# Which queue issues the two transfers that regroup the keys: SyncE or GpSimd

## The chip, the cores and the metric

The kernel runs on one core of a Trainium2 chip. The core's engines work side by side, each through its own list of instructions in order: TensorE (PE, with its weight loads PEld), VectorE (DVE), ScalarE (ACT), GpSimd (POOL) and SyncE (SP), which here only issues transfers. Any of SyncE, ScalarE and GpSimd can issue a transfer (DMA); an issue that has to wait holds up all that stands behind it on its engine. The metric is the device time in microseconds of one execution, of which the span from the first to the last instruction is nearly all.

## What is computed

A decaying linear attention, whose output goes through two gated feed-forward layers (the second behind an RMS norm). The core of the reference:

```python
# attention: q, k, v, a_re, a_im are (4, 8, 768, 48)
mag = np.sqrt(a_re * a_re + a_im * a_im)
scale = np.minimum(mag, 0.999) / (mag + 1e-06)
a_re_n, a_im_n = (a_re * scale, a_im * scale)
for t in range(S):
    ar, ai = (a_re_n[:, :, t, :, None], a_im_n[:, :, t, :, None])
    new_re = ar * S_re - ai * S_im
    new_im = ar * S_im + ai * S_re
    kv = np.einsum('bhd,bhe->bhde', k[:, :, t], v[:, :, t])
    S_re, S_im = (new_re + kv, new_im)
    y[:, :, t] = np.einsum('bhd,bhde->bhe', q[:, :, t], S_re)
# a layer: x (3072, 384), w_gate and w_val (384, 1536), w_out (1536, 384), float64 in memory
g = x @ w_gate
silu = g * (1.0 / (1.0 + np.exp(-g)))
return (silu * (x @ w_val) @ w_out).astype(np.float32)
# the second layer's x is first x / sqrt(mean(x * x) + 1e-06) * rms_g
```

## The kernel before, in words

The 768 steps are cut into 6 blocks of 128, the 8 heads into pairs: 24 groups of one block and two heads, numbered block by block. Two groups that follow one another are a pair and share their decays. For a pair, `e1` and `scan` turn a_re and a_im (tile `aar`) into running products of the decays; for a group, `e2a` and `e2b` multiply the queries (`qt`) and the keys divided by the products (`kt`, L664, on VectorE). ScalarE makes the logarithms and exponentials for this (L488, L489, L631, L632), and the copies of transposes.

On TensorE a group is `pe_att`: transposes of kt and qt (`tp`, L689), scores (`sp`, L704), the output (`yp`, L721 and L726) and, as late work behind the next group's scores, the new state (`zp`, L745 and L747). For zp the keys are wanted with time on the partitions. `regroup` makes that: it stores kt to a scratch tensor `kd` in HBM (L672, two buffers) and loads it in the other order into `ktok` (L673, one buffer). kd waits for kt; ktok waits for kd to land and for the zp that read ktok before. The values `vt` (two buffers) are loaded at L453, the output goes by L736 from `yt` into `xf`.

When the four groups of a block are done, `layer1` runs the first feed-forward layer for its 512 columns: projections (`gv`, L361, 9 matmuls each), Silu on ScalarE (`h`, L370), product on VectorE (L384), rounding and remainder (`hh` L385, `hl` L393), and the output (`acc`, L797). Each weight tile comes by L328 into `wraw`, is narrowed from float64 by VectorE (L59 to L61) and split into two parts by ScalarE, in the first layer with TensorE's help (`wl`, L336 and L337). The second layer (`o`, L921) follows for all 3072 rows, its weights being loaded and narrowed while the last block's first layer runs.

The order is set in two steps. The tables T_E1 to T_WF at the top give each task a due time, and `in_order` lists the pieces by it. A scheduler then places each instruction on its engine's list by an estimate of when its operands are there; so a change of one transfer's engine can move instructions on all engines. ScalarE needs another table for Silu than for logarithm and exponential; a table load is set in wherever the list goes from one to the other. Before the change every transfer is issued by SyncE, but for the stores of x1d (L805) and two of the last outputs, which ScalarE issues. GpSimd fills masks at the start (up to L313) and one tile of ones between the layers (L955).

Of the kernel before, what the change touches and what calls it, by code (L numbers as in the profile page):

```python
# [261 lines left out]
def decay_attention_two_ffn(ctx: ExitStack, tc: tile.TileContext, q, k, v, a_re, a_im,  # L262
                            wg, wv, wo, w2g, w2v, w2o, rms_g, out):
    nc = tc.nc
    V, A, T, G, SY = nc.vector, nc.scalar, nc.tensor, nc.gpsimd, nc.sync
# [23 lines left out]
    with ExitStack() as fast:  # L289
# [346 lines left out]
        def e2b(i, s):  # L636
            gr = groups[i]
            b = gr.blk
            U, C, el = b.U, b.C, b.el
            half = i % 2  # L640
            o = {}

            def qq(c):
                def go():
                    if c == 0:
                        o["q"] = ap1.tile([128, 4 * G2 * 2 * D], F32, tag="qt", name="qt", bufs=BUFS["qt"])[:, :2 * el].rearrange(
                            "p (u g c d) -> p u g c d", u=U, g=G2, c=2)
                        o["k"] = ap1.tile([128, 4 * G2 * 2 * D], F32, tag="kt", name="kt", bufs=BUFS["kt"])[:, :2 * el].rearrange(
                            "p (u g c d) -> p u g c d", u=U, g=G2, c=2)
                        qkn[i] = (o["q"], o["k"])  # L650
                    V.tensor_tensor(o["q"][:, :, :, c, :], qk[i][:, 0, :el].rearrange("p (g u d) -> p u g d", g=G2, u=U),
                                    s["a"][:, c].rearrange("p u (g d) -> p u g d", g=G2), op=ALU.mult)
                return go

            def nw():
                m2, w0, t = s["q2"][:, 0], s["q2"][:, 1], s["tt"][:, 768:768 + el]
                V.tensor_tensor(t, m2, w0, op=ALU.mult)
                V.scalar_tensor_tensor(w0, t, 2.0, w0, op0=ALU.subtract, op1=ALU.mult)
                wv_ = w0.rearrange("p (u g d) -> p u g d", g=G2, u=U)
                V.tensor_tensor(wv_, wv_, qk[i][:, 1, :el].rearrange("p (g u d) -> p u g d", g=G2, u=U), op=ALU.mult)  # L660

            def kk(c):
                def go():
                    V.tensor_tensor(o["k"][:, :, :, c, :], s["q2"][:, 1].rearrange("p (u g d) -> p u g d", g=G2, u=U),  # L664
                                    s["a"][:, c].rearrange("p u (g d) -> p u g d", g=G2), op=ALU.mult)
                return go

            def regroup():
                kt = ap2.tile([128, B, G2, 2, D], F32, tag="ktok", name="ktok", bufs=BUFS["ktok"])
                ktok[i] = kt  # L670
                kd = dram.tile([128, U, G2 * 2 * D], F32, tag=f"kd{U}", name="kd", bufs=2)
                SY.dma_start(out=kd, in_=o["k"].rearrange("p u g c d -> p u (g c d)"))  # L672
                SY.dma_start(out=kt[:C].rearrange("p b g c d -> p b (g c d)"),  # L673
                             in_=kd.rearrange("(b r) u x -> (r u) b x", b=B))

            return [(1, qq(0)), (1, qq(1)), (3, nw), (1, kk(0)), (1, kk(1)), (0.1, regroup)]

        def pe_att(i):
# [351 lines left out]
```

## Time and profile before

| | us |
|---|---|
| median of 3 runs (1218.2 to 1222.41) | 1219.62 |
| the profiled execution | 1217.24 |
| its span | 1215.5 |
| TensorE busy in the span | 1133.2 |
| VectorE, ScalarE, GpSimd busy | 777.0, 672.3, 1.5 |
| mean granted TensorE clock | 0.986 of full |

Durations in rows come from the profiled execution. In a row of waits stand the engine and line that waited, whom for, the total in us, how often and the longest; the one waited for is the one that came last. In a row of a timeline stand the start in us, the time in us, engine, line, operation, operands, and the idle time ahead in square brackets with what ended it. A row of the windows gives one stretch.

### The profile page before, as it was taken

Reading aid. Unit: us, or ns where it says so; the run is one execution under the profiler, and the core shown is the slowest. Engines: PE = TensorE matmul, PEld = TensorE weight load, DVE = VectorE, ACT = ScalarE, POOL = GpSimd, SP = SyncE. Lnnn points to the kernel's source line nnn. Section 1 sums busy time; section 2 is a strip of 40 time slices with the busy share of each in tenths; the row PEclk is TensorE's granted clock in tenths of the full one; section 3 lists DMA queues with packets and bytes.
Section 4 is the critical chain, followed back from the end, with each engine's and each line's share of the span. In section 5 each row is a group of like instructions: output and inputs, shape, how many; then the busy total and the mean of one; then the engine's idle time right before and its main releaser. Section 6 shows DMA issues by size and latency. Waiting matters only on the chain.

```text
span 1215.5 us, 16686 instructions
## 1 busy us (share of the span) xinstructions
PE 1133.2 (93%) x6098; PEld 944.7 (78%) x6098; DVE 777.0 (64%) x1711; ACT 672.3 (55%) x1167; POOL 1.5 (0%) x12
## 2 busy tenths in 40 slices
PE   2468979999999999999999999999999999999997
PEld 1246767788888888888878877888888888888886
DVE  5988999989888697888754488842432424224222
ACT  5666979876677656675364688742421424214211
POOL 0000000000000000000000000000000000000000
PEclk9988989999999999999999999999999999999998
DMA  6255454442423224222313244400010000000000
GB/s 168 85 145 143 116 154 141 123 118 66 119 76 90 75 60 123 57 82 70 95 59 98 79 130 145 129 26 28 1 52 1 26 27 1 26 1 1 27 1 29
DMA packets 105514, 90.84 MB, mean 75 GB/s; under 512 B 34000, under 2 KB 92368, under 8 KB 105424
## 3 DMA queue, kind: packets, MB, share of 16 engines
q1 hardware_dynamic: 102544, 84.58, 24.4%
q10 hardware_dynamic: 2880, 5.11, 1.1%
q8 instruction: 50, 0.82, 0.3%
q14 instruction: 40, 0.33, 0.1%
HBM read 66.06 MB, written 18.87 MB: 70 GB/s over the span
## 4 chain that ended last, share of the span: by engine, by line
PE 72%; ACT 11%; DVE 8%; DMA 4%; issue 2%; SPq 1%; ACTq 0%; DVEq 0%
PE gv L361 39%; PE o L921 12%; PE acc L797 8%; PE sp L704 4%; PE tp L689 3%; DMA wraw<-in_moe_w_gate_dram 2%; ACT T L695 2%; PE zp L745 2%; PE yp L721 2%; PE yp L726 1%; ACT L425 1%; ACT T L692 1%; DMA wraw<-in_moe_w_val_dram 1%; SPq L430 1%; ACT w L332 1%
## 5 line engine op out<-in xcount | busy, mean ns | idle before, releaser
L361 PE MATMUL gv<-xh,w 128*128 128x512 f32 x1728 | 569.2, 394 | 0.3 <-ACT h L370 0.3
L361 PEld LDWEIGHTS gv<-xh,w 128*128 128x128 f32 x1728 | 324.2, 188 | 67.8 <-ACT h L370 1.3
L361 PE MATMUL gv<-xl,w 128*128 128x512 f32 x864 | 339.1, 393 | 0.0
L384 DVE TENSOR_TENSOR gv<-h,gv 128x512 f32<-128x512 f32 (+1 forms) x145 | 100.1, 691 | 217.0 <-PE gv L361 211.3
L370 ACT ACTIVATE h<-gv 128x512 f32<-128x512 f32 x144 | 85.9, 597 | 185.2 <-PE gv L361 184.6
L361 PEld LDWEIGHTS gv<-xl,w 128*128 128x128 f32 x864 | 162.5, 188 | 31.4 <-issue 0.5
L385 ACT ACTIVATE hh<-gv 128x512 fp32r<-128x512 f32 (+1 forms) x145 | 85.7, 591 | 158.5 <-DVE gv L384 157.8
L393 DVE TENSOR_TENSOR hl<-gv,hh 128x512 fp32r<-128x512 f32 (+1 forms) x145 | 99.3, 685 | 103.1 <-PE o L921 70.8
L797 PE MATMUL acc<-hh,w 128*128 128x512 f32 x432 | 148.5, 398 | 2.6 <-ACT hh L385 2.6
L921 PE MATMUL o<-w,hh 128*128 128x384 f32 x576 | 146.5, 337 | 0.4 <-ACT x1s L803 0.4
L921 PEld LDWEIGHTS o<-w,hh 128*128 128x128 f32 x576 | 105.6, 188 | 5.9 <-ACT x1s L803 0.7
L921 PE MATMUL o<-w,hl 128*128 128x384 f32 x288 | 96.8, 340 | 0.9 <-DVE hl L393 0.9
L797 PEld LDWEIGHTS acc<-hh,w 128*128 128x128 f32 x432 | 80.3, 188 | 21.0 <-ACT hh L385 4.1
L797 PE MATMUL acc<-hl,w 128*128 128x512 f32 x216 | 86.3, 399 | 0.7 <-DVE hl L393 0.4
L336 PE MATMUL wl<-wy,ident 128*128 128x384 f32 x72 | 39.6, 639 | 42.3 <-DVE wy L61 30.7
L695 ACT ACTIVATE T<-tp 96x512 f32<-96x512 f32 x48 | 52.7, 1097 | 42.6 <-PE tp L689 42.1
L704 PEld LDWEIGHTS sp<-T,T 96*128 96x128 f32 x384 | 51.4, 204 | 22.8 <-ACT T L692 21.4
L704 PE MATMUL sp<-T,T 96*128 96x128 f32 x384 | 57.4, 296 | 9.6 <-ACT T L692 9.3
L921 PEld LDWEIGHTS o<-w,hl 128*128 128x128 f32 x288 | 53.5, 188 | 2.9 <-DVE hl L393 2.9
L336 PEld LDWEIGHTS wl<-wy,ident 128*128 128x128 f32 x72 | 14.2, 231 | 50.8 <-DVE wy L61 36.1
L370 ACT ACT_TABLE_LOAD x38 | 48.8, 1283 | 3.4 <-PE gv L361 2.7
L797 PEld LDWEIGHTS acc<-hl,w 128*128 128x128 f32 x216 | 40.6, 188 | 11.0 <-DVE hl L393 2.9
(134 smaller groups left out, 1502.3 us busy)
## 6 DMA issues: line engine op xcount, KB each, us to landing
wraw<-in_moe_w_gate_dram SPq DMA_DIRECT2D x24, 384.0 KB, 3.6
wraw<-in_moe_w_val_dram SPq DMA_DIRECT2D x24, 384.0 KB, 3.4
wraw<-in_moe_w_out_dram SPq DMA_DIRECT2D x24, 384.0 KB, 3.2
kd<-kt SPq DMA_DIRECT2D x24, 384.0 KB, 2.5
ktok<-kd SPq DMA_DIRECT2D x24, 384.0 KB, 3.6
aar<-in_a_re_dram SPq DMA_DIRECT2D x48, 96.0 KB, 2.4
aar<-in_a_im_dram SPq DMA_DIRECT2D x48, 96.0 KB, 2.7
qk<-in_q_dram SPq DMA_DIRECT2D x96, 48.0 KB, 2.3
```

Of the source, the lines that this page charges most:

```text
L336: T.matmul(ps[:, :384], ident, y, start=True, stop=False)
L361: T.matmul(ps[:, :N], w[:, a, i + c, :], x()[b][:, c, :N], start=(n == 0), stop=(n == 8))
L370: A.activation(h[:, :N], st[f, 0][:, :N], AF.Silu)
L384: V.tensor_tensor(t[:, z], st[f, "h"][:, z], st[f, 3][:, z], op=ALU.mult)
L385: A.activation(hh[:, z], t[:, z], AF.Copy)
L393: V.tensor_tensor(hl[:, z], st[f, "t"][:, z], st[f, "hh"][:, z].bitcast(F32), op=ALU.subtract)
L689: T.transpose(ps[0:96, u * 128:u * 128 + 128], s[:, u, h].rearrange("p c d -> p (c d)"), ident)
L695: A.activation(t[:, :N].rearrange("p (b r u) -> p u b r", u=U, b=B), ps[0:96, :N].rearrange("p (u b r) -> p u b r", u=U, b=B), AF.Copy)
L704: T.matmul(ps[:C, bb * C:bb * C + C], o[h, 1][:, bb], o[h, 0][:, :, bb, :], start=True, stop=True)
L721: T.matmul(dst, vt[i][:C, col:col + 64], o[h, "p"][:C, bb * C:bb * C + C].rearrange("p (u r) -> p u r", u=U), start=True, stop=not inter)
L797: T.matmul(acc[e][:, :N], w[:, a, 6 + e, :], hs_[c][:, :N], start=(f == 0 and n == 0), stop=(f == NF - 1 and n == 2))
L921: T.matmul(acc[m][:, :DM], hs_[c][:, m * 128:m * 128 + 128], w[:, a, 6:9, :].rearrange("p c e -> p (c e)"), start=(f == 0 and x == 0), sto ...
```

## The change

Both transfers of `regroup` are put on GpSimd's queue (G) in place of SyncE's (SY).

```diff
                 kd = dram.tile([128, U, G2 * 2 * D], F32, tag=f"kd{U}", name="kd", bufs=2)
-                SY.dma_start(out=kd, in_=o["k"].rearrange("p u g c d -> p u (g c d)"))
-                SY.dma_start(out=kt[:C].rearrange("p b g c d -> p b (g c d)"),
+                G.dma_start(out=kd, in_=o["k"].rearrange("p u g c d -> p u (g c d)"))
+                G.dma_start(out=kt[:C].rearrange("p b g c d -> p b (g c d)"),
                              in_=kd.rearrange("(b r) u x -> (r u) b x", b=B))
```

The scheduler places instructions anew. SyncE's list is the same up to the loads of the queries for group 2, where the first kd and ktok stood. Before (x2, x3, x4 are the batches of one load; aar belongs to the pair of groups 4 and 5):

```order
L328 DMA wraw<-in_moe_w_val_dram 128x3x256
L430 DMA qk<-in_q_dram 32x2x192 x2
L672 DMA kd<-kt 128x768
L430 DMA qk<-in_q_dram 32x2x192 x2
L430 DMA qk<-in_k_dram 32x2x192
L673 DMA ktok<-kd 128x4x192
L430 DMA qk<-in_k_dram 32x2x192 x3
L430 DMA aar<-in_a_re_dram 32x4x192 x4
L430 DMA aar<-in_a_im_dram 32x4x192 x2
L736 DMA xf<-yt 48x512 x2
```

The same place on SyncE with the change:

```order
L328 DMA wraw<-in_moe_w_val_dram 128x3x256
L430 DMA qk<-in_q_dram 32x2x192 x4
L430 DMA qk<-in_k_dram 32x2x192 x4
L430 DMA aar<-in_a_re_dram 32x4x192 x4
L430 DMA aar<-in_a_im_dram 32x4x192 x4
L736 DMA xf<-yt 48x512 x2
```

The two transfers of the keys are gone from it, and all eight loads of the decays stand ahead of the store of xf. On GpSimd, between the last mask and the memset of L955, the pairs of kd and ktok now stand, 24 of each (the first rows):

```order
L313 AFFINE_SELECT mask_100<-mask_100 128x128
L672 DMA kd<-kt 128x768
L673 DMA ktok<-kd 128x4x192
L672 DMA kd<-kt 128x768
L673 DMA ktok<-kd 128x4x192
```

Before, L955 came right behind that mask. On ScalarE the third place is the exponentials of group 17, near the end of a block's first layer. Before:

```order
L623 ACTIVATE e2t<-an 128x768
L425 ACT_TABLE_LOAD
L631 ACTIVATE e2t<-e2t 128x384
L803 ACTIVATE x1s<-acc_3951 128x4x128
L632 ACTIVATE e2t<-e2t 128x384
```

And with the change:

```order
L370 ACT_TABLE_LOAD
L370 ACTIVATE h<-gv 128x512
L425 ACT_TABLE_LOAD
L385 ACTIVATE hh<-gv 128x512
L370 ACT_TABLE_LOAD
L370 ACTIVATE h<-gv 128x512
L631 ACT_TABLE_LOAD
L631 ACTIVATE e2t<-e2t 128x384
L385 ACTIVATE hh<-gv 128x512
L632 ACT_TABLE_LOAD
```

Silu (L370) now falls between the steps of the group's logarithm and exponential, with a table load at each turn. In the whole program ScalarE has 88 table loads before and 100 with the change.

## Rows read from the trace of the kernel before

**Rows 1.** The page: each engine's busy time, its share of the span, its instructions.
```profile
PE 1133.2 (93%) x6098; PEld 944.7 (78%) x6098; DVE 777.0 (64%) x1711; ACT 672.3 (55%) x1167; POOL 1.5 (0%) x12
```

**Rows 2.** Windows: stretch, length, busy PE, PEld, DVE, ACT, POOL; clock, DMA share, GB/s
```profile
0.00:45.00 45.00, 9.37 (x15) 4.14 (x15) 31.87 (x89) 26.39 (x56) 1.32 (x11) 1.00 0.44 115
45.00:210.00 165.00, 135.07 (x730) 102.39 (x729) 149.57 (x372) 126.34 (x267) 0.00 (x0) 0.92 0.48 139
210.00:635.00 425.00, 420.30 (x2662) 348.01 (x2661) 351.40 (x843) 284.74 (x406) 0.00 (x0) 1.00 0.32 89
635.00:765.00 130.00, 126.45 (x576) 103.03 (x575) 86.89 (x167) 89.49 (x204) 0.20 (x1) 1.00 0.37 112
765.00:1215.50 450.50, 441.96 (x2124) 387.16 (x2122) 157.31 (x243) 145.33 (x236) 0.00 (x0) 0.99 0.07 23
```

**Rows 3.** Waits of TensorE from 45 to 210 us: total, times, longest.
```profile
PE tp L689 <- DVE kt L664: 7.0, 4, 3.1
PE wl L336 <- DVE wy L61: 6.6, 5, 2.4
PE tp L689 <- DVE X L462: 5.9, 1, 5.9
```

**Rows 4.** Waits of TensorE from 210 to 640 us.
```profile
PE sp L704 <- ACT T L692: 3.7, 12, 0.6
PE tp L689 <- ACT T L695: 0.6, 2, 0.3
```

**Rows 5.** Waits of SyncE's queue over the whole span.
```profile
SPq L328 <- DVE wy L61: 138.4, 51, 14.5
...
SPq L673 <- PE zp L747: 93.0, 19, 14.4
SPq L672 <- DVE kt L664: 49.0, 15, 11.3
```

**Rows 6.** Timeline of SyncE's queue, 47 to 71 us.
```profile
47.99 0.35 SPq L672 DMA_DIRECT2D kd<-kt  x1
...
50.64 0.38 SPq L673 DMA_DIRECT2D ktok<-kd  x1
...
69.53 0.90 SPq L430 DMA_DIRECT2D aar<-in_a_im_dram  x2
```

**Rows 7.** Groups of VectorE's instructions by form: count, busy us, mean ns of one.
```profile
L783 DVE TENSOR_TENSOR xl<-xf,xh 128x512 fp32r<-128x512 f32 x18 | 12.2, 685 | 0.5 <-ACT xh L782 0.5
...
L494 DVE TENSOR_TENSOR e1w<-e1w,an 128x768 f32<-128x768 f32 x12 | 11.4, 952 | 3.8 <-ACT e1w L493 3.8
```

**Rows 8.** Timelines of SyncE's queue and TensorE, 315 to 330 us.
```profile
315.73 0.38 SPq L673 DMA_DIRECT2D ktok<-kd  x1
316.16 1.06 SPq L453 DMA_DIRECT2D vt<-in_v_dram  x2
...
329.07 0.80 PE L745 MATMUL zp<-vt,ktok 128*96 128x48 f32 x8
```

**Rows 9.** Groups of ScalarE's instructions, 210 to 640 us: count, busy us, mean ns.
```profile
L370 ACT ACT_TABLE_LOAD x27 | 34.6, 1283 | 3.2 <-PE gv L361 2.7
L425 ACT ACT_TABLE_LOAD x24 | 30.8, 1283 | 0.4
```

**Rows 10.** DMA issues: count, KB each, median us from issue to landing.
```profile
kd<-kt SPq DMA_DIRECT2D x24, 384.0 KB, 2.5
ktok<-kd SPq DMA_DIRECT2D x24, 384.0 KB, 3.6
```

**Rows 11.** Timelines: VectorE's keys of group 11, and TensorE's transposes of them.
```profile
320.63 1.02 DVE L664 TENSOR_TENSOR kt<-e2t,an 128x384 f32<-128x384 f32 x2
322.06 0.60 PE L689 MATMUL tp<-ident,kt 128*96 128x128 f32 x4
```

**Rows 12.** Groups of VectorE's instructions: L59 and L60, mean ns of one.
```profile
L59 DVE TENSOR_SCALAR wy<-wraw 128x384 uint32<-128x384 uint32 x72 | 25.5, 356 | 16.3 <-DMA wraw<-in_moe_w_gate_dram 12.6 <-DMA wraw<-in_moe_w_out_dram 2.4 <-DMA wraw<-in_moe_w_val_dram 0.9
L60 DVE SCALAR_TENSOR_TENSOR wy<-wraw,wy 128x384 uint32<-128x384 uint32 x72 | 39.8, 555 | 0.8
```

## The prediction

> **What bounds the kernel now.** I read the profile from the outside in: the windows by stage, the waits of TensorE in the stages where it idles, then the waits of the queue that loses the two transfers. TensorE is busy 441.96 of the last 450.50 us and 420.30 of the 425 us between 210 and 635 us; it idles 35.6 us before 45 us, 29.9 us between 45 and 210 us and 3.6 us between 635 and 765 us [rows 2]. So the end is set by TensorE's own work plus what it loses in the first 210 us. In 45 to 210 us VectorE is busy 149.57 of 165 us and ScalarE 126.34 [rows 2]: TensorE there waits for what VectorE and ScalarE make, the keys (7.0 us on L664, and 5.9 us in one piece that the view names after X at L462, which ends beside L664), and the narrowed weights (6.6 us) [rows 3]. After 210 us the largest are 3.7 and 0.6 us [rows 4]. No row of TensorE's waits names a transfer. GpSimd has 1.5 us of work in the whole span [rows 1], all but 0.2 us of it in the first stage [rows 2].
>
> SyncE is another matter: it waits much. L673 waited 93.0 us for zp, in 19 pieces, and L672 49.0 us for the keys; but L328 waited 138.4 us for VectorE to free a weight buffer [rows 5]. A queue that waits is not a queue that is late: what counts is who needs the transfers behind it.
>
> **The change part by part.** *The issues.* SyncE loses 24 issues of 0.35 us and 24 of 0.38 us [rows 6], 17.5 us in all, and the waits ahead of them; the same 48 transfers go to GpSimd, where nothing else is queued between the masks and the memset of L955. That memset and the test of the flag after it now stand behind the last ktok; the memset's reader is the second layer's first norm, behind the whole last block of the first layer: nothing.
>
> *What moves up behind them.* The first kd stood at 47.99 and the first ktok at 50.64 us; the loads behind them move up by their issue and wait, some 2.3 us, and the two a_im loads that stood at 69.53 us, behind an xf store, now stand ahead of it, right behind the first two [rows 6]. That lets VectorE take the next pair's e1 steps earlier, but it takes them ahead of nearer work: in the new order L494 and L499 (0.95 us each, by L494's row) stand before the keys of group 2, and one L783 (0.69 us) behind [rows 7]: +1.2 us. Counted in the same way for group 3 it is +0.6, for group 4 +2.0, for group 5 -0.4, for groups 6 and 7 -0.2 us and for group 8 nothing different. VectorE works in order and is over 90% busy, so the sum of work ahead of the keys is when they come. The loss at group 4 is inside the 5.9 us for which TensorE later waits for group 5 anyway [rows 3], and at group 5 VectorE is level again. By this engine the first stage costs **-0.2 us**.
>
> *A wait stays where it was.* The ktok load of 315.73 us is followed at once by the vt loads and the xf stores [rows 8]. Those wait for the same group's matmuls and copies: vt's buffer is free only when yp and zp have read it, and xf needs yt. So SyncE still stops near there, now at L453 or L736; of 93.0 us of waiting most changes its name. I count no gain from it, because TensorE waits for no load.
>
> *The activation tables.* The order is built with other arrival times, and ScalarE's instructions fall differently: 100 table loads against 88 in all the program. One costs 1283 ns [rows 9]. One of the twelve stands ahead of the exponentials of group 4 (counted up to its L632), a second ahead of group 6's; ten come from group 14 on, most of them after 400 us, where Silu now falls between the logarithm and the exponential. The first two are 2.6 us on an engine that is 77% busy in that stage [rows 2]: all of it if ScalarE is the later of the two engines, nothing if VectorE is. I take the middle of -0.2 and +2.6, **+1.2 us**. The ten later ones are 12.8 us on an engine busy 284.74 of 425 us; at the upper end all of it delays TensorE, at the lower nothing. The 51 loads that stand in 210 to 640 us now [rows 9] live beside TensorE waits of 4.3 us [rows 4], 0.08 us for each, and this row is the nearest: 10 x 0.08 = **+0.8 us**.
>
> *The transfer by GpSimd.* No row shows a transfer that GpSimd issues. From SyncE kd lands in 2.5 and ktok in 3.6 us [rows 10]. Who waits for them: ktok is needed by zp alone (L745), and its single buffer is free only when the zp before it is done. The closest pair of zp: the ktok between them is issued at 315.73 us, would land at 319.3 us, and zp reads it at 329.07 us [rows 8]; 9.7 us are to spare, and at the other 18 pairs more. Faster landing gains nothing, and slower landing costs nothing up to 9.7 us more. Above that each further microsecond is paid at up to 19 places. I take **0**; the other end is a rival below. The Trainium skill (DMA: Bandwidth & Descriptors, Specifications) gives about 1 us to the first byte on the GpSimd path and 0.6 us on the SyncE path; as an estimate from that page 48 x 0.4 = 19 us if every transfer were on the path, and nothing by the slack above. No run here shows either latency.
>
> **The sum.** 1.2 + 0.8 = +2.0 us. The profiled execution took 1217.24 us, 1215.5 of it the span, so 1219.2 us by it; the median of the three runs shown is 1219.62 us, 2.4 us above the profiled one. On the scale of the median: 1219.6 + 2.0 = **1221.6 us**. A measurement of this kernel can tell about 0.3%, 3.7 us, from no change; the forecast lies within it.
>
> **The rivals.**
> *Slower, by the order.* The keys come hardly ahead of their transposes: group 11's end at 321.65 us and are read at 322.06 [rows 11]. Up to there TensorE has under half a microsecond in hand at most groups, so a chain of ScalarE that gets 2.6 us longer can reach TensorE several times, and the ten later loads stand in front of Silu, whose product TensorE needs next. With all of the twelve loads on the path it is 15.4 us; a third to a half of that, 5 to 8 us, is what I would expect if this happens: 1225 to 1230 us, say 1227. For it: the count of loads, and two engines that are 91 and 77% busy beside each other up to 210 us. Against it: from 330 us on TensorE has work of the first layer in its own queue between the groups, and hardly waits now. It decides once loads that follow one another delay Silu beyond what TensorE holds between a projection and its product.
>
> *Slower, by GpSimd.* A transfer whose issue to landing on GpSimd takes over 3.6 + 9.7 = 13.3 us stops TensorE at the closest zp, and the next ones after it. At 15 us it would be under 2 us at each of a few pairs, at most 10 us in all: about 1230 us. A second form lies on VectorE. L59 takes 356 ns for 384 elements and L60 555 ns for as many [rows 12], so L59 runs in a faster form than its neighbours; if that form and GpSimd's writing of descriptors shut each other out, VectorE stands still in the stage in which it is the bound: 14 transfers before 210 us, with 0.4 us (one L59) at each, are 5 us of VectorE and up to 1226 us. The Trainium skill (SBUF — State Buffer, section SBUF: two separate sides, the box on the "DVE blocks DMA" trap) states that GpSimd can't write descriptors while VectorE runs an operation that uses both of its ports, and in its section Who interferes with whom that whoever comes second waits for the whole instruction. The trace agrees only so far as L59's 356 ns go; no row has both engines at work.
>
> *Faster.* SyncE without 48 issues and two waits for each group brings loads forward at a place where the chain needs them. A weight load may stand behind a ktok that waits for zp, as the vt loads do [rows 8]. If the narrowed weights come earlier, the 6.6 us in L336's row shrink, and the 5.9 us before group 5 may as well: 4 to 8 us of the 29.9 us, 1212 to 1216, say 1214 us. Against it: VectorE is busy 91% of that stage, and earlier data don't make it faster.
>
> **How the numbers follow.** Forecast, within 0.3% (1216 to 1223.3 us): 0.44. Slower by the order: 0.32. Slower by GpSimd: 0.09. Faster: 0.15. So faster 0.15, same 0.44, slower 0.41. The range for 8 in 10 leaves about one in ten at either end: the lower end cuts the faster rival near its price, 1214.5; the upper takes in twice the middle price of the slower ones, 1231. The likeliest case alone has 1216 to 1223.3.
>
> **What would show it.** ScalarE's table loads in the new profile (88 to 100 in the program, fewer executed) and TensorE's waits after 210 us: below 6 us the forecast holds, over 10 us the first rival. DMA issues: kd and ktok under 10 us from issue to landing, and no wait of L745 for ktok. SyncE's waits: L673 and L672 gone, L453 and L736 larger. VectorE: a mean of L59 of 356 ns as before; 500 ns or more would be the shut-out. TensorE's idle time in 45 to 210 us: 29.9 us, give or take 3. A granted clock other than 0.92 there would add a cause that I don't count: TensorE ran for parts of that stage at the lower level.

## The result, and the profile with the change

| | before | with the change |
|---|---|---|
| median, us (runs) | 1218.91 (4) | 1228.76 (4) |
| lowest and highest, us | 1216.65, 1222.41 | 1228.2, 1230.14 |
| ratio, 95% interval | | 1.0083 (1.0067 to 1.0099) |
| span of the profiled execution, us | 1215.5 | 1227.0 |

The change costs 9.9 us. That lies inside the range of the prediction (1214.5 to 1231 us), but not where its forecast lay (1221.6 us, within 0.3%); it is nearest to the first rival, "slower, by the order", which was put at 1227 us.

First the row of the page on the engines, which answers [rows 1], and the windows that answer [rows 2] (columns as there):

```profile
PE 1138.7 (93%) x6098; PEld 944.9 (77%) x6098; DVE 777.3 (63%) x1711; ACT 691.1 (56%) x1179; POOL 33.3 (3%) x60
```

```profile
45.00:210.00 165.00, 134.43 (x717) 100.27 (x715) 147.55 (x367) 128.70 (x267) 8.57 (x13) 0.92 0.50 139
210.00:635.00 425.00, 416.27 (x2594) 341.99 (x2594) 348.90 (x840) 292.99 (x410) 21.87 (x33) 1.00 0.30 85
```

GpSimd has 48 instructions more and 31.8 us more work; ScalarE has 12 more (the table loads) and 18.8 us more. TensorE has as many matmuls as before and 5.5 us more busy time. In the first stage its idle time is 30.6 us (29.9 before) at the same granted clock of 0.92.

The waits of TensorE from 210 to 640 us, which answer [rows 4] (columns: who waits, for whom, us in total, times, longest):

```profile
PE sp L704 <- ACT T L692: 5.9, 14, 1.6
PE gv L361 <- ACT h L370: 1.6, 1, 1.6
PE tp L689 <- ACT T L695: 0.6, 2, 0.3
PE gv L361 <- ACT xh L782: 0.5, 1, 0.5
PE acc L797 <- DVE hl L393: 0.2, 1, 0.2
```

Together 8.8 us, and all but 0.2 of it for ScalarE. Before it was 4.6 us: the 4.3 us of [rows 4] and one row more of the same view of the kernel before:

```profile
PE gv L361 <- ACT h L370: 0.3, 1, 0.3
```

The waits of SyncE's queue over the whole span, which answer [rows 5], and the issues of the two transfers, which answer [rows 10]:

```profile
SPq L328 <- DVE wy L61: 154.3, 53, 14.3
...
SPq L453 <- PE zp L747: 106.8, 19, 13.3
SPq L736 <- ACT yt L728: 69.4, 13, 29.2
```

```profile
kd<-kt POOLq DMA_DIRECT2D x24, 384.0 KB, 3.0
ktok<-kd POOLq DMA_DIRECT2D x24, 384.0 KB, 4.6
```

The waits of L673 and L672, 142.0 us, are gone. The 106.8 us of L453 are new, and L736 waits 27.1 us longer for yt (42.3 before): nearly the whole wait stayed and changed its name.

**Where the time went** is not read from these sums. The kernel has a mark that says it better: when a block's first layer is done, ScalarE copies the first part of acc out (L803). The first of these rows, of the kernel before and with the change:

```profile
253.84 1.10 ACT L803 ACTIVATE x1s<-acc 128x512 f32<-128x512 f32 x1 [0.43 <-PE acc L797]
```

```profile
256.69 1.11 ACT L803 ACTIVATE x1s<-acc 128x512 f32<-128x512 f32 x1 [0.44 <-PE acc L797]
```

The distance from one such mark to the next is a block's length. In kernels whose lists are alike in a block it agrees to about 0.1 us in the second, third and fifth block (the second: 107.39, 107.45, 107.40, 107.45 and 107.49 us in five of the kernels of the table), so it tells far smaller things than a timed run. The sixth is less steady (77.5 to 78.4 us with the lists of before), and so is the fourth with the lists of the change (110.0 us, and 109.1 in e2). The first block's end is not steady either: with the lists of the kernel before it fell between 252.4 and 254.0 us in four profiles, with those of the changed kernel between 254.5 and 256.7 us in five. The table gives the marks of all kernels, worked out from the rows of L803 of their timelines; the experiments follow in the next section. The marks are those of one execution, the ratio is that of all; for e8, e9 and e10 the execution with the marks was the slowest.

| kernel | 1st ends | 2nd | 3rd | 4th | 5th | 6th | ratio, 95% interval |
|---|---|---|---|---|---|---|---|
| before | 253.8 | 107.4 | 105.1 | 106.4 | 102.2 | 77.9 | 1 |
| with the change | 256.7 | 108.4 | 106.4 | 110.0 | 103.6 | 78.8 | 1.0083 (1.0067 to 1.0099) |
| e1 lists of before, GpSimd issues | 254.0 | 107.5 | 105.1 | 106.4 | 102.1 | 77.8 | 1.0008 (0.9995 to 1.0021) |
| e2 lists of the change, SyncE issues | 255.2 | 108.5 | 106.4 | 109.1 | 103.6 | 78.0 | 1.0079 (1.0066 to 1.0092) |
| e3 ScalarE's list of before alone | 259.8 | 107.6 | 105.0 | 106.4 | 102.2 | 77.6 | 1.0046 (1.0028 to 1.0063) |
| e4 change, six places mended | 254.6 | 108.4 | 106.1 | 106.5 | 103.6 | 77.6 | 1.0049 (1.0033 to 1.0066) |
| e5 e1, twelve table loads added | 252.4 | 107.4 | 110.7 | 115.2 | 103.9 | 78.1 | 1.0127 (1.0104 to 1.0149) |
| e6 before, three places mended | 253.3 | 107.8 | 105.0 | 105.9 | 102.1 | 77.5 | 0.9996 (0.9983 to 1.0008) |
| e7 change up to the first mark | 255.1 | 107.5 | 105.1 | 106.3 | 102.2 | 78.2 | 1.0029 (1.0017 to 1.0040) |
| e8 e1, SyncE's list of the change | 269.6 | 107.5 | 105.1 | 106.5 | 102.1 | 78.4 | 1.0106 (1.0087 to 1.0126) |
| e9 only ktok on GpSimd | 266.0 | 109.9 | 104.2 | 106.4 | 102.1 | 78.2 | 1.0093 (1.0076 to 1.0109) |
| e10 only kd on GpSimd | 268.3 | 114.6 | 102.3 | 106.4 | 102.2 | 77.6 | 1.0132 (1.0106 to 1.0158) |
| e11 e4, one Silu earlier | 254.5 | 108.2 | 106.1 | 106.4 | 103.6 | 77.5 | 1.0045 (1.0030 to 1.0059) |
| e12 e7, weight loads ahead | 256.8 | 107.5 | 105.1 | 106.3 | 102.2 | 78.2 | 1.0024 (1.0015 to 1.0032) |

With the change 2.8 us are lost up to the first mark of this profile, and 1.0, 1.3, 3.6, 1.4 and 0.9 us in the blocks behind it; the second layer adds 0.4 us. In e2, with the same lists, the fourth block loses 2.7 us and the sixth 0.1. The second layer, 462.6 to 463.6 us in the other profiles, takes 464.9 us in e2 and 465.2 in e9; why is open.

### The profile page after: what moved, and what is told of

Its sections match the earlier page's. It is cut to its first block, busy times and chain, and to the rows that moved or that the text cites. A ratio compares the mean times of both kernels' runs of the same rounds, so it can differ in the third digit from the quotient of the medians.

```text
span 1227.0 us, 16726 instructions
## 1 busy us (share of the span) xinstructions
PE 1138.7 (93%) x6098; PEld 944.9 (77%) x6098; DVE 777.3 (63%) x1711; ACT 691.1 (56%) x1179; POOL 33.3 (3%) x60
## 3 DMA queue, kind: packets, MB, share of 16 engines
q0 software_dynamic: 4608, 18.88, 4.5%
## 4 chain that ended last, share of the span: by engine, by line
PE 69%; ACT 13%; DVE 9%; DMA 5%; issue 2%; SPq 1%; ACTq 0%; DVEq 0%
PE gv L361 37%; PE o L921 12%; PE acc L797 8%; PE sp L704 4%; ACT T L695 3%; DMA wraw<-in_moe_w_gate_dram 2%; PE zp L745 2%; PE tp L689 2%; PE yp L721 2%; PE yp L726 1%; ACT T L692 1%; ACT L370 1%; ACT L425 1%; DMA wraw<-in_moe_w_val_dram 1%; ACT h L370 1%
## 5 line engine op out<-in xcount | busy, mean ns | idle before, releaser
L384 DVE TENSOR_TENSOR gv<-h,gv 128x512 f32<-128x512 f32 (+1 forms) x145 | 100.0, 690 | 226.8 <-PE gv L361 206.2
L370 ACT ACTIVATE h<-gv 128x512 f32<-128x512 f32 x144 | 85.8, 596 | 175.8 <-PE gv L361 175.0
L336 PE MATMUL wl<-wy,ident 128*128 128x384 f32 x72 | 39.4, 636 | 42.8 <-DVE wy L61 30.3
L695 ACT ACTIVATE T<-tp 96x512 f32<-96x512 f32 x48 | 52.7, 1098 | 21.7 <-PE tp L689 21.0
L336 PEld LDWEIGHTS wl<-wy,ident 128*128 128x128 f32 x72 | 14.1, 229 | 51.1 <-DVE wy L61 36.8
```

The source lines that it names most:

```text
L336: T.matmul(ps[:, :384], ident, y, start=True, stop=False)
L370: A.activation(h[:, :N], st[f, 0][:, :N], AF.Silu)
L384: V.tensor_tensor(t[:, z], st[f, "h"][:, z], st[f, 3][:, z], op=ALU.mult)
L695: A.activation(t[:, :N].rearrange("p (b r u) -> p u b r", u=U, b=B), ps[0:96, :N].rearrange("p (u b r) -> p u b r", u=U, b=B), AF.Copy)
```

## The experiments

The change does two things at once: it gives two transfers to another engine, and it makes the scheduler place instructions anew on every list. The first theory (A) was that the new places cost the time and the issue by GpSimd costs nothing; the rival (B) that GpSimd's transfers cost it, by later landing or by standing in VectorE's way. To part them, the order of an engine's list was held by edges between neighbours that set the order of issue and wait for nothing. This stands at the end of the kernel's body; a table gives each list by the place of its instructions in the text:

```python
            _row = [_mine[j + o] for j, o in enumerate(_off)]
            for _x, _y in zip(_row, _row[1:]):
                tc.add_manual_dep(_y, _x.name, mybir.DependencyInfo(
                    mybir.DependencyClass.NoSync, mybir.DependencyReason.DATA), reason="order")
```

The traces have 84 table loads in the kernel before and 96 with the change; the prediction's 88 and 100 are those in the program, of which four did not run.

### One half at a time

**e1**: GpSimd issues, the lists of before.

```diff
-                SY.dma_start(out=kd, ...
-                SY.dma_start(out=kt[:C]...
+                G.dma_start(out=kd, ...
+                G.dma_start(out=kt[:C]...
...
+ORDER = {"PE": <before>, "DVE": <before>, "Activation": <before>, "SP": <before, less the 48>, ...}
```

> GpSimd issues both transfers of the keys, as in the changed kernel, but the order of TensorE's, VectorE's, ScalarE's and SyncE's other instructions is held at that of the kernel before, by edges that set order of issue alone. Theory A (the new order of the lists costs the time, the issue by GpSimd nothing): the time of the kernel before, ratio 1.000, within 0.3%, 84 to 88 table loads, and ktok's landing still near 4.6 us. Theory B (the transfers on GpSimd cost it: later landing, or VectorE hindered while GpSimd describes them): ratio about 1.008, as the changed kernel. A share of each would lie between, by its size.

Measured: 1.0008 (0.9995 to 1.0021), no difference that can be told, and each block as long as before to 0.1 us. ktok landed in 4.3 us.

**e2**: SyncE issues, the lists of the change.

```diff
                 SY.dma_start(out=kd, ...
                 SY.dma_start(out=kt[:C]...
...
+ORDER = {"PE": <change>, "DVE": <change>, "Activation": <change>, "SP": <change, with the 48 put in>}
```

> The other half: SyncE issues both transfers, as in the kernel before, but the order of TensorE, VectorE, ScalarE and of SyncE's other transfers is held at that of the changed kernel; the two transfers stand on SyncE's list where the changed program as a whole has them. Theory A (order): ratio 1.008, 1.005 to 1.011, TensorE's waits for T L692 and h L370 as in the changed kernel (12.7 and 1.6 us). Theory B (GpSimd): ratio 1.000, within 0.3%.

Measured: 1.0079 (1.0066 to 1.0092), the whole loss without one transfer on GpSimd. The waits are those of the change, too: 12.4 us for T at L692 over the span, 1.6 us for h at L370. Theory B falls; what remains is which of the new places cost the time.

**e3**: GpSimd issues, ScalarE's list alone is held.

```diff
+ORDER = {"Activation": <before>}
```

> GpSimd issues both transfers, ScalarE's list alone is held at the order of the kernel before, and with it its number of table loads; the scheduler is free in the rest. Theory A1 (within the order it is ScalarE's list, with its twelve more table loads, that costs the time): ratio 1.000 to 1.003. Theory A2 (the moved instructions of TensorE and VectorE cost it, the table loads lie hidden or cost the 2.0 us that the prediction gave them): ratio 1.005 to 1.008. Theory B (GpSimd): 1.008.

Measured: 1.0046 (1.0028 to 1.0063), between the two. The blocks tell why. From the first mark on they are as long as before: with ScalarE's list of before the scheduler makes nearly the other lists of before as well (221 of 1711 places differ on VectorE, and none of TensorE's behind 311 us). The whole loss, 5.9 us in this profile, lies ahead of the first mark, where most of those differences are. It did not come in every execution: five of the six took 1223.3 to 1223.9 us and one 1217.34, and why is open. So the later blocks follow from ScalarE's list, but the experiment doesn't say whether by its table loads or by other places. ScalarE's list of the one kernel with TensorE's and VectorE's of the other would say it; there is no such run.

### What a table load costs

In the fourth block of the changed kernel ScalarE's timeline reads (columns: start us, us, engine, line, operation):

```profile
477.36 1.28 ACT L370 ACT_TABLE_LOAD   x1
...
479.27 1.28 ACT L425 ACT_TABLE_LOAD   x1
...
481.18 1.28 ACT L370 ACT_TABLE_LOAD   x1
...
483.09 1.28 ACT L631 ACT_TABLE_LOAD   x1
...
485.42 1.28 ACT L632 ACT_TABLE_LOAD   x1
...
487.14 1.08 ACT L695 ACTIVATE T<-tp 96x512 f32<-96x512 f32 x1
488.24 1.28 ACT L370 ACT_TABLE_LOAD   x1
489.54 0.60 ACT L370 ACTIVATE h<-gv 128x512 f32<-128x512 f32 x1
490.03 0.58 ACT L692 ACTIVATE T<-tp 96x512 f32<-96x512 f32 x1
```

Six loads in 12.2 us, with no idle time between the rows, and the copies of the transposes (T, L695 and L692) at the end of the row. TensorE's timeline at the same place:

```profile
488.43 0.61 PE L797 MATMUL acc<-hh,w 128*128 128x512 f32 x2
490.67 1.16 PE L704 MATMUL sp<-T,T 96*128 96x128 f32 x8 [1.62 <-ACT T L692]
```

It ran out of work of the layer and stopped for 1.62 us until L692 was done.

**e4** puts six such places right: a Silu that stands between the logarithm and the exponential goes behind, or the load goes behind the Silu. The third of the six, on ScalarE's list:

```diff
-L370 ACT_TABLE_LOAD
-L370 ACTIVATE h<-gv 128x512
-L425 ACT_TABLE_LOAD
-L385 ACTIVATE hh<-gv 128x512
-L370 ACT_TABLE_LOAD
-L370 ACTIVATE h<-gv 128x512
-L631 ACT_TABLE_LOAD
-L631 ACTIVATE e2t<-e2t 128x384
-L385 ACTIVATE hh<-gv 128x512
-L632 ACT_TABLE_LOAD
+L370 ACTIVATE h<-gv 128x512
+L385 ACTIVATE hh<-gv 128x512
+L370 ACTIVATE h<-gv 128x512
+L425 ACT_TABLE_LOAD
+L631 ACTIVATE e2t<-e2t 128x384
+L385 ACTIVATE hh<-gv 128x512
 L632 ACTIVATE e2t<-e2t 128x384
```

> GpSimd issues, and all lists stand as in the changed kernel, but for six places on ScalarE's list in the blocks from the third on: where a Silu (L370) stands between a table load or logarithm and the exponential that belongs to it, the Silu is put behind the exponential, or the load behind the Silu. That takes 14 table loads out (96 to 82). Theory A1 (the table loads between them cost the loss after the first block, 0.4 to 0.7 us each where ScalarE's copies are what TensorE waits for): ratio 1.000 to 1.004. Theory A2 (the loads lie hidden at the 0.08 us each of the prediction, other moves in the lists cost the time): ratio 1.006 to 1.008. The loss in the first 254 us, 2.8 us, should stay in either.

Measured: 1.0049 (1.0033 to 1.0066), a gain of 0.0034 or 4.1 us on the change, between the two forecasts. The blocks show that both were right in different places. The fourth block, 110.0 us with the change, is 106.5, level with the kernel before: its loss was the table loads there, together with the places of Silu that make them needed (the edit takes both away). The change has 20 loads in this block, e4 has 11 and the kernel before 14: the six new ones cost 3.6 us (2.7 in e2), 0.45 to 0.6 us each, and going three below the number of before gains nothing more. The third block loses three loads and gains 0.3 us. The fifth has four loads more with the change than before; e4 takes two of them out and the block stays as long. The second, where no load was added, keeps its 1.0 us. The sixth is 1.2 us shorter, but that one isn't steady. The same place with the edit:

```profile
477.46 0.60 ACT L370 ACTIVATE h<-gv 128x512 f32<-128x512 f32 x1 [0.70 <-PE gv L361]
478.08 1.28 ACT L425 ACT_TABLE_LOAD   x1
479.38 0.53 ACT L631 ACTIVATE e2t<-e2t 128x384 f32<-128x384 f32 x1
480.25 0.60 ACT L385 ACTIVATE hh<-gv 128x512 fp32r<-128x512 f32 x1 [0.34 <-DVE gv L384]
```

ScalarE now waits for the others at two of the four rows, where it had a queue of work before.

**e5** adds loads and moves nothing: at the six pairs that the change tears apart, Silu's table and then the other's are loaded once more.

```diff
             pre = A.preload_act_table_set("natural_log_exp_and_others")
...
+            if len(calls) - 1 in TWICE:
+                pair = [A.preload_act_table_set(x).ins for x in ("silu_and_others", "natural_log_exp_and_others")]
```

> GpSimd issues, all lists stand as in the kernel before, and at the six pairs that the changed kernel tears apart two more table loads (Silu's and back) are set ahead of the logarithm: twelve loads more, nothing moved. Theory A1: 0.4 to 0.7 us a load, ratio 1.004 to 1.007 against the kernel before. Theory A2 (hidden, 0.08 us a load): ratio 1.001, not told from the first experiment's 1.0008.

Measured: 1.0127 (1.0104 to 1.0149), 14.5 us above e1 and far above both theories: 1.2 us for each load of 1.28 us, as if nothing hid them. The profile has a second cost in it, in the fourth block. Right ahead of the third mark ScalarE loads three tables in a row (the edit moves the lines of this kernel on by one to seven; L789 is L782 elsewhere):

```profile
466.13 1.28 ACT L427 ACT_TABLE_LOAD   x1
467.42 2.57 ACT L431 ACT_TABLE_LOAD   x2
```

A split of x (xh, here L789) comes late behind them, TensorE stops, and what it does next is slow. Its timeline, then the windows from there, of the third block and of the fourth (column before the last two: the granted clock):

```profile
473.54 2.01 PE L361 MATMUL gv<-xh,w 128*128 128x512 f32 x4 [2.29 <-ACT xh L789]
```

```profile
473.50:478.00 4.50, 4.46 (x13) 3.55 (x14) 1.71 (x4) 3.85 (x5) 0.56 (x1) 0.62 0.55 208
...
359.77:470.43 110.66, 108.26 (x681) 90.43 (x680) 86.12 (x206) 76.48 (x101) 5.30 (x8) 1.00 0.28 79
470.43:585.63 115.20, 108.11 (x650) 89.37 (x649) 87.54 (x208) 75.13 (x103) 5.28 (x8) 0.96 0.25 69
```

Four matmuls take 1.80 us up to the next row at 475.34, 0.45 us each, where at full clock one takes 0.23: the lower of the two levels, 1.2 GHz. In the fourth block the loads' price is thus mixed with the clock's. The third block has six of the twelve loads at full clock and is 5.6 us longer than in e1, the fifth has two and is 1.8 us longer: 0.9 us a load. At these places most of a load's time reaches the end, and a stop of TensorE can cost more than its length.

**e6** takes loads out of the kernel before, which has three such places of its own (six loads); SyncE issues.

```diff
 L631 ACTIVATE e2t<-e2t 128x384
-L370 ACT_TABLE_LOAD
-L370 ACTIVATE h<-gv 128x512
-L632 ACT_TABLE_LOAD
-L632 ACTIVATE e2t<-e2t 128x384
+L632 ACTIVATE e2t<-e2t 128x384
+L370 ACT_TABLE_LOAD
+L370 ACTIVATE h<-gv 128x512
```

> SyncE issues, all lists as in the kernel before, but for three places on ScalarE's list where the kernel before too has a Silu between a logarithm and its exponential: the Silu goes behind. Six table loads less (84 to 78). Theory A1: 2.4 to 4.2 us less, ratio 0.9965 to 0.998. Theory A2: 0.5 us less, ratio 1.000, within 0.1%.

Measured: 0.9996 (0.9983 to 1.0008). Six loads less, 7.7 us of ScalarE, give at most 2 us and by the middle of the interval 0.5. With two loads less in each of three blocks, the fourth gains 0.6 us, the third nothing, and the second loses 0.4. By the whole time the loads lay hidden here, as theory A2 said. The price of a load is thus one of its place: none that can be told here, about 0.5 us in the fourth block of the change, 0.9 us in e5.

The Trainium skill (ScalarE: Activation LUTs, Table sets: the hidden batching unit) says to batch activations by table set rather than by function. The fourth block of e4 agrees, 3.5 us shorter than with the change; e6 shows the rule kept better than before and no gain that can be told.

**e11** tests the second block, which has no more loads than before and is 1.0 us longer. Its profile has one large wait, for a Silu that stands behind three steps of the attention. On ScalarE's list of e4:

```diff
 L692 ACTIVATE T_2507<-tp 96x512
+L370 ACT_TABLE_LOAD
+L370 ACTIVATE h<-gv 128x512
 L623 ACTIVATE e2t<-an 128x768
 L695 ACTIVATE T_2521<-tp 96x4x128
-L370 ACT_TABLE_LOAD
-L370 ACTIVATE h<-gv 128x512
```

> The changed kernel with the six places mended, and one Silu more moved: the first Silu of the second block, which stands behind three copies and Squares of the attention in the changed kernel and made TensorE wait 1.59 us, is put ahead of two of them. If the place of that Silu makes the second block longer (108.4 us in place of 107.4): block back to 107.2 to 107.7 and ratio 1.0035 to 1.0045. If not, block at 108.4 and ratio 1.0049 as without it.

Measured: the block has 108.2 us in place of 108.4, ratio 1.0045 (1.0030 to 1.0059). The theory falls. TensorE's timeline with the change, then in e11:

```profile
267.84 0.50 PE L361 MATMUL gv<-xh,w 128*128 128x512 f32 x1 [1.59 <-ACT h L370]
```

```profile
267.69 0.50 PE L797 MATMUL acc<-hh,w 128*128 128x512 f32 x1 [1.63 <-ACT hh L385]
```

The wait for h is gone, and 1.63 us for hh stand in its place a few matmuls on. In e11 hh waited 0.22 us for VectorE's product (L384). The product's row in e11, then in the kernel before:

```profile
266.32 0.69 DVE L384 TENSOR_TENSOR gv<-h,gv 128x512 f32<-128x512 f32 x1
```

```profile
261.84 0.69 DVE L384 TENSOR_TENSOR gv<-h,gv 128x512 f32<-128x512 f32 x1
```

In e11 h is done at 263.27 us, and the product stands on VectorE's list behind L626, an L507 and the two L651 of the next queries. In the kernel before h is done at 261.61 us, the product follows at once, and L651 comes 4 us later. So VectorE's new order is a candidate for this block, with ScalarE's; no experiment moved it, and what makes the block longer stays open.

### The first block

**e7** holds the lists of the change up to the first mark and those of before from there.

```diff
+ORDER = {"PE": <change up to the first L803, then before>, "DVE": <same>, "Activation": <same>, ...}
```

> GpSimd issues, the lists stand as in the changed kernel up to the end of the first block's layer (254 us), and as in the kernel before from there. If the loss of each stretch is its own and nothing is given back later: the 2.8 us of the first stretch and no more, ratio 1.002 to 1.0035. If the profile of the changed kernel misled on the first stretch and all loss belongs to the later blocks: 1.000. If a late start is made up later, since TensorE is not bound by it: 1.000 too, with the first block ending 2.8 us late in its profile.

Measured: 1.0029 (1.0017 to 1.0040), that is 3.5 us, and the blocks behind the mark are as long as before to 0.1 us, but for the unsteady sixth (78.2). So the first block's loss is its own, nothing of it is given back, and the other 6.6 us (1.0083 less 1.0029) belong to what comes later. TensorE's granted clock doesn't order the first block's ends: from 45 to 250 us it was 0.93 before (253.8 us), 0.91 in e1 (254.0), 0.96 in e2 (255.2) and 0.90 in e7 (255.1).

**e8** is e1 with one list more from the change, SyncE's: the loads that moved up when the two transfers left.

```diff
-ORDER = {..., "SP": <before, less the 48>, ...}
+ORDER = {..., "SP": <change>, ...}
```

> GpSimd issues, SyncE's list stands as in the changed kernel (the loads of queries, keys and decays moved up), the lists of TensorE, VectorE and ScalarE as in the kernel before: the first experiment with SyncE's order added. If the loads that move up cost or give nothing, as the prediction has it (-0.2 us): ratio 1.000 to 1.0015, first block's end within 1 us of 254. If they crowd the first stage (the transfers of GpSimd and the weights share the queues' bandwidth there) and make its loss: 1.0025 to 1.003, as in the experiment that held the first block's lists alone.

Measured: 1.0106 (1.0087 to 1.0126), at least as much as the change itself, and all of it ahead of the first mark (269.6 us). Neither side of the expectation had this. SyncE's timeline of e8, then that of before for the same loads:

```profile
161.21 0.33 SPq L430 DMA_DIRECT2D aar<-in_a_re_dram  x1
161.65 0.84 SPq L328 DMA_DIRECT2D wraw<-in_moe_w_gate_dram  x1
...
173.99 0.94 SPq L453 DMA_DIRECT2D vt<-in_v_dram  x2
175.02 0.45 SPq L328 DMA_DIRECT2D wraw<-in_moe_w_val_dram  x1
```

```profile
157.78 0.38 SPq L328 DMA_DIRECT2D wraw<-in_moe_w_val_dram  x1
158.26 1.65 SPq L430 DMA_DIRECT2D aar<-in_a_re_dram  x3
...
163.96 1.06 SPq L453 DMA_DIRECT2D vt<-in_v_dram  x2
```

A weight load that stood ahead of the decays and values stands behind both now, and both wait: 11.2 us for VectorE to free aar's buffer, 8.8 us for zp to free vt's. ScalarE pays, whose list is in the old order (its waits, 45 to 254 us):

```profile
ACT w L332 <- DMA wraw<-in_moe_w_val_dram: 10.4, 1, 10.4
...
ACT w L332 <- DMA wraw<-in_moe_w_gate_dram: 4.9, 2, 4.7
```

A load that moves up takes its wait along, and holds up what it has passed.

**e12** asks whether this is also the loss of the changed kernel, in which the same weight load stands behind vt (issued at 166.99 us, right after vt at 165.94). In e7, four weight loads go ahead of the waiting loads on SyncE's list; two of them:

```diff
-L430 DMA aar<-in_a_re_dram 32x4x192 x4
-L328 DMA wraw<-in_moe_w_gate_dram 128x3x256
+L328 DMA wraw<-in_moe_w_gate_dram 128x3x256
+L430 DMA aar<-in_a_re_dram 32x4x192 x4
...
-L453 DMA vt<-in_v_dram 128x4x48 x2
-L328 DMA wraw<-in_moe_w_val_dram 128x3x256
+L328 DMA wraw<-in_moe_w_val_dram 128x3x256
+L453 DMA vt<-in_v_dram 128x4x48 x2
```

> The experiment that holds the changed kernel's lists through the first block and the lists of before behind it, with one edit on SyncE's list: four weight loads (L328) go ahead of the loads of decays and values (L430, L453) that stand ahead of them in the changed kernel's list and wait there for VectorE or for zp (the last weight load by 6.5 us). If weight loads held up on SyncE make the first block's loss: ratio 1.000 to 1.0015, the first block's end at 252.5 to 254.2, ScalarE's wait for the weights of L332 gone. If the new places on TensorE, VectorE and ScalarE make it: ratio 1.002 to 1.0035 as without the edit.

Measured: 1.0024 (1.0015 to 1.0032). ScalarE's wait for that load, from 45 to 254 us in e7 and then in e12:

```profile
ACT w L332 <- DMA wraw<-in_moe_w_val_dram: 3.0, 1, 3.0
```

```profile
ACT w L332 <- DMA wraw<-in_moe_w_val_dram: 0.8, 2, 0.6
```

2.2 us of waiting are gone and the time is the same within the two intervals: with the lists of the change the end doesn't hang on this wait. So weight loads held up on SyncE don't make the first block's loss. The new places on TensorE, VectorE and ScalarE are left, and SyncE's other moves, which no run takes apart. Which of them it is stays open; ScalarE has 80.4 us of work in the 90 us from 120 to 210 us of e7 where it had 77.5 before, with two more table loads up to the first mark, but no experiment took these two out alone.

### The transfers one by one

**e9** and **e10** give one transfer of the two to GpSimd and leave the scheduler free.

```diff
                 SY.dma_start(out=kd, ...
-                SY.dma_start(out=kt[:C]...
+                G.dma_start(out=kt[:C]...
```

> The load of ktok alone is issued by GpSimd, the store of kd stays on SyncE, the scheduler is free. The lists that result hold 85 table loads, one more than before, but with 20 in place of 15 within the first block and 12 in place of 14 in the third. Theory A (time follows the lists, and a table load costs most where ScalarE has no room): first block 3 to 6 us later, later blocks as before, ratio 1.002 to 1.005. Theory B (a cost of GpSimd's transfers): half of the changed kernel's, 1.004, spread over all blocks.

Measured: 1.0093 (1.0076 to 1.0109); the first mark 12.1 us late, the second block 2.5 us longer, the third 0.9 us shorter, the rest as before.

```diff
-                SY.dma_start(out=kd, ...
+                G.dma_start(out=kd, ...
                 SY.dma_start(out=kt[:C]...
```

> The store of kd alone is issued by GpSimd, the load of ktok stays on SyncE, the scheduler is free. The lists that result hold 95 table loads: 24 in place of 15 within the first block, 19 in place of 16 in the second, 11 in place of 14 in the third, and as before in the rest. Theory A: first block 5 to 11 us later, second block up to 3 us longer, the blocks after it as before, ratio 1.005 to 1.012. Theory B: about 1.004, spread over all blocks.

Measured: 1.0132 (1.0106 to 1.0158); the first mark 14.4 us late, the second block 7.2 us longer, the third 2.8 us shorter, the rest as before. Half of the change costs as much as all of it (e9) or more (e10), and mostly in the blocks whose lists came out otherwise; where they are as before, half of GpSimd's transfers run and cost nothing. Theory A named the first block for both and the second for e10; it missed the second block of e9, and its sizes were too small (3 to 6 us for 12.1 in e9's first block, 5 to 11 us for 14.4 in e10's). A count of loads doesn't price a block: in the traces 16 stand ahead of the first mark before, 18 with the change, 21 in e9 and 27 in e10, and the second block of e9 is longer with two loads less than before.

No version here is faster than the kernel before; e1 and e6 are level with it.

## Why the prediction was right or wrong

The time came inside the range, but by the room that was given to the first rival: the forecast's own sum had +2.0 us, and 9.9 were measured.

**What bounds the kernel** was right in the engine and too coarse in the place. TensorE's own work sets the end, and no transfer of the keys is waited for. But that TensorE "hardly waits now" was read as room for ScalarE. From the first mark to the last, blocks 2 to 6, the time grew by 8.3 us. The windows of that stretch, before and with the change (columns as in [rows 2]):

```profile
253.84:752.78 498.94, 492.59 (x2910) 407.12 (x2909) 389.20 (x887) 328.44 (x523) 0.20 (x1) 1.00 0.31 90
```

```profile
256.69:763.89 507.20, 495.85 (x2907) 406.61 (x2906) 389.62 (x885) 343.93 (x533) 21.30 (x33) 1.00 0.31 88
```

TensorE is idle 5.0 us longer, and busy 3.3 us longer with three matmuls fewer at the same clock. The likely reason for the second is that stops too short to be listed as waits look like work, since the ends of matmuls are modelled; no run shows it.

**The issues** at nothing, **GpSimd's transfer** at 0, and that **the wait stays where it was**: right, by e1 and e2, and by the rows of L453. The transfers land 0.5 and 1.0 us later than from SyncE [rows 10], against 9.7 us to spare. The Trainium skill (DMA: Bandwidth & Descriptors, Specifications) gives about 1 and 0.6 us to the first byte for the two paths, 0.4 us apart; the landings here differ by 0.5 us for kd and by more for ktok (1.0, and 0.7 in e1). L59 took 354 ns by the median of its 72 (356 before), and none over 365 (columns: shortest, median and longest in ns, first and last start in us):

```profile
L59 DVE TENSOR_SCALAR wy<-wraw x72: 320/354/365, 9.9 to 795.2; 128x384 uint32<-128x384 uint32 x72
```

So the rival by GpSimd, at 0.09, did not come in either form.

**What moves up behind the issues**, -0.2 us: wrong as a way of counting. It took VectorE's list alone as the measure of when keys come. e8 shows that SyncE's new order by itself moves the first block's end by 15.7 us in its profile (1.0106, or 12.9 us, by all its runs) when the other lists don't follow it, and e12 that the waits of weight loads in it cost nothing that can be told when they do. What the first block costs is a property of the four lists together.

**The two table loads of the first stage**, +1.2 us: this was the middle of -0.2 and +2.6, so it is all that the sum had for the first block; e7 measured 3.5 us (2.1 to 4.9). By how much the two loads share in it is open.

**The ten later loads**, +0.8 us: this is the term that failed most. It stood for all that comes behind the first mark, which is 6.6 us (1.0083 less the 1.0029 of e7). 3.6 us (2.7 in e2) are lost in the fourth block, where six of the ten loads stand: about 0.5 us each where the sum had 0.08. The 0.08 was an average over 51 loads that the order had put where ScalarE had room; e6 found such loads in the kernel before, and six of them cost nothing that can be told. With those that came new, six stand in a row ahead of the copies that TensorE needs. The rest is 1.0, 1.3 and 1.4 us in the second, third and fifth blocks. In the second and third no load was added. In the fifth four were; taking two out again gained nothing (e4), and the other two were not tried. So the cause of this part stays open. e3 ties these blocks only to what follows from ScalarE's list.

**The choice among the cases** followed from that term. The first rival named the mechanism that came in the fourth block, with its deciding point (loads that follow one another delay Silu, though it was the copies L692 behind them that TensorE waited for). Its price of 5 to 8 us is below the 9.9 measured; on the prediction's scale it is 1224.6 to 1227.6 us, where the text has 1225 to 1230. It had 0.32 against 0.44, because "hardly waits now" was held against it. The test it set, under 6 us of waits after 210 us for the forecast and over 10 for the rival, gave 8.8: it decided nothing.

**Faster**, 0.15: the freed queue brought no narrowed weights that TensorE could use. Its waits for them up to the first mark (L336 for L61) are 30.3 us, and 30.7 before.

## What to carry to other kernels

Where a scheduler places the instructions, the change of one transfer's engine is first a new order on every list, and here that was all of the cost that can be told (e1 1.0008, e2 1.0079); hold the lists at the old order before judging the edit. Price a new wait or load by what stands behind it on its engine's list, not by the average over those already there, and look for several in a row. Measure by marks between which the work is the same: here TensorE's idle time told 5.0 of the 8.3 us that the marks showed.

## What the runs showed of the hardware

GpSimd is busy with an issue where SyncE's queue is not counted as busy (columns: count, busy us, mean ns):

```profile
L673 POOL DMA_DIRECT2D ktok<-kd x24 | 18.2, 757 | 251.7 <-PE zp L747 237.5 <-DMA kd<-kt 5.5 <-DMA ktok<-kd 4.7
L672 POOL DMA_DIRECT2D kd<-kt x24 | 13.6, 566 | 362.2 <-DVE kt L664 285.6 <-DVE wy L59 56.9 <-DVE X L551 19.6
```

The issues took 566 and 757 ns there, against 0.35 and 0.38 us in the rows of SyncE's queue [rows 6]. And the same bytes went in fewer packets. The first queue before, then the two queues with the change (packets, MB, share of 16 engines):

```profile
q1 hardware_dynamic: 102544, 84.58, 24.4%
```

```profile
q1 hardware_dynamic: 86416, 65.70, 19.8%
q0 software_dynamic: 4608, 18.88, 4.5%
```

The 48 transfers were 16128 packets, 336 each, from SyncE and are 4608, 96 each, from GpSimd. They landed later all the same. The other thing not expected is in e5: after a stop of TensorE of 2.29 us the granted clock of the next 4.5 us was 0.62, with matmuls at half their pace, and 0.96 over that whole block, where e1 had 1.00 from 466.5 to 572.9 us.
